# Four early loads of a fused attention and long-convolution kernel issued from ScalarE's queue

## The chip, the cores and the metric

The kernel runs on one core of a Trainium2 chip. A core has five engines, each with an instruction queue of its own that runs in order: TensorE (PE, with its weight loads as PEld), VectorE (DVE), ScalarE (ACT), GpSimd (POOL) and SyncE (SP, which only issues transfers here). Sixteen DMA engines move data between HBM and the core's memory. The metric is the device time of one execution in microseconds (us), as the median of several runs.

## The reference: what is computed

Two stages follow each other. The first is a linear attention with a decaying state, for 4 batches (B), 8 heads (H), 768 steps (S) and head size 48 (D):

```python
for t in range(S):
    kt, vt, rt, wt = k[:, :, t], v[:, :, t], r[:, :, t], w[:, :, t]
    cur = np.einsum('bhd,bhe->bhde', u[None] * kt, vt)
    y[:, :, t] = np.einsum('bhd,bhde->bhe', rt, state + cur)
    state = wt[:, :, :, None] * state + np.einsum('bhd,bhe->bhde', kt, vt)
```

Its output, laid out as 4 x 768 x 384, goes through the second stage:

```python
x1, x2, x3 = np.split(x @ w_proj, 3, axis=-1)
X2 = np.fft.rfft(x2, n=S, axis=1) * np.fft.rfft(filter_fft, n=S, axis=0)[None]
y = x1 * np.fft.irfft(X2, n=S, axis=1) * x3
out = y @ w_out
```

The inputs r, k, v and w are float32 in HBM, laid out batch, head, step, head size.

## The kernel before, in words

The 768 steps of each batch are cut into six chunks of 128 steps (L), which makes 24 chunks in all, numbered 0 to 23; chunks 0 to 5 belong to batch 0. For each chunk four loads bring r, k, v and w as 128 x 384 float32 (192 KB each, 8 x 128 pieces of 192 bytes) into rings of six buffers: ldr, ldk, ldv, ldw. All of them are made by `op_ld` (line 449, the issue at line 452).

What is done to a chunk c, with the names of the schedule:

- `lw` (line 457, ACT): the logarithm of w. `cs` and `ce` (lines 464 and 468, PE): its running sums, inclusive and exclusive of the step itself, as products with triangular masks. `en`, `eq`, `ph` (lines 483 to 495, ACT): the exponentials of those sums.
- `kh` and `q` (lines 501 and 504, DVE or POOL): k times en, and r times eq, into the buffer qk. `rk` (line 507): r times k.
- `rt` and `rT`, `tqk` and `tT` (PE, then DVE or ACT): transposes of rk and of qk and their copies out of PSUM. `sc` (line 601, PE): the scores of a chunk. `mt` (line 612, DVE): their mask. `cp` and `cc`, `vc`: the term with u. `kv` and `S` (lines 619 and 631): the state that goes on to the next chunk. `y`, `xn`, `yt`, `xT`: the output of the attention and its transpose.
- `um`, `ub`, `ubd`, `uc`, `rku`: what is made of u, whose 1.5 KB are loaded by `ldu`.

The second stage does the Fourier transforms as products with matrices of sines. These are computed at the start: the angles by `ang` and `and` (lines 329 and 347, DVE), the sines by `sin` (line 355, ACT), which loads ACT's table of sines before and the table of logarithms and exponentials after. The filter's spectrum follows (`fs`, `fd`, `hf`, `H`, `hg`), and then, batch by batch, projections (`p1`, `x2`, `p3`), spectra (`f`), products (`ur`, `ui`, `pp`), inverses (`iE`, `iO`, `iP`), gates (`g`, `yy`) and the output product (`po`, `o`), stored by `st`.

The order of all work is written out by hand in the string ORDER (lines 42 to 141). Each word names an engine and an operation: `A:` ACT, `V:` DVE, `P:` PE, `G:` POOL, `S:` SyncE. `emit` (line 864) takes the words one by one, so that each engine's queue has its own words in the order of the string. A number behind `@` is the PSUM bank, and one behind `+` a number of matmuls on a tile of zeros that PE runs ahead of the operation. The framework adds the semaphore waits. ACT's queue begins with

```python
A:tLn0 ... A:lw0 ... A:lw1 ... A:lw2 ... A:en1 A:eq0 ... A:lw4 ... A:en2 ... A:eq2 ... A:eq1 A:ph2 A:en0 ... A:ph1 ... A:sin ... A:v0 ... A:eq4 ... A:ph0 ... A:lw3 ... A:uc
```

where `tLn0` (line 352) loads ACT's table of logarithms. SyncE's queue begins with

```python
S:ldw0 S:ldk2 S:ldw1 S:ldr3 S:ldw2 S:ldu S:ldr0 S:ldw4 S:ldk1 S:ldk0 S:ldr1 S:ldw6 S:ldv2 S:ldr2 S:ldv0 S:ldk3 S:ldw3 S:ldr4 ...
```

and DVE's first products come in the order q0, rk0, kh0, q1, kh1, with the last of the angles between q0 and rk0. All transfers, the weights, the filter and the stores too, are issued by SyncE.

Of the kernel before, what the change touches and what calls it, by code (L numbers as in the profile page):

```python
# [19 lines left out]
B, H, S, D = 4, 8, 768, 48  # L20
# [19 lines left out]


ORDER = """
A:tLn0 S:ldw0 G:iota S:ldk2 S:ldw1 S:ldr3 G:mx V:late G:mi V:ang2 S:ldw2 G:uh A:lw0 S:ldu V:ang1
S:ldr0 P:ce0@0+2 S:ldw4 G:id A:lw1 V:ang0 S:ldk1 P:cs1@1+3 S:ldk0 P:cs0@2 G:nyq A:lw2 S:ldr1
V:and1 A:en1 P:ce2@3+4 A:eq0 S:ldw6 P:um@4 P:cs2@5 V:q0 P:ce1@1 A:lw4 V:and2 S:ldv2 A:en2 V:and0
A:eq2 P:ce4@5 S:ldr2 A:eq1 A:ph2 A:en0 V:rk0 P:ub@3 A:ph1 S:ldv0 A:sin V:kh0 P:rt0@2 V:q1
P:tqk0@1+1 S:ldk3 V:kh1 V:rT0 V:tT0 S:ldw3 P:tqk1@2 P:sc0@8+1 S:ldr4 V:rk2 G:q2 S:ldw5 G:rk1
# [97 lines left out]
def kernel(  # L145
# [12 lines left out]
    nc = tc.nc  # L158
# [83 lines left out]
    nyq = consts.tile([L, NT], FP32)  # L242
# [42 lines left out]
    def bi(c):  # L285
        return divmod(c, NCH)
# [162 lines left out]
    def op_ld(e, x, c):  # L449
        b, ci = bi(c)  # L450
        src = dict(w=w, k=k, r=r, v=v)[x]
        nc.sync.dma_start(  # L452
            out=ld[x][c % 6],
            in_=src[b, :, ci * L:ci * L + L, :].rearrange("h t d -> t h d"),
        )
# [476 lines left out]
```

## Time and profile before

| | |
|---|---|
| median of 3 runs | 156.67 us (156.21 to 157.68) |
| profiled execution, time | 157.1 us |
| profiled execution, span of its instructions | 155.4 us |
| mean granted TensorE clock | 0.973 of full speed |
| DMA moved | 28.98 MB, mean 186 GB/s over the span |
| loads of r, k, v, w | 24 of each, 192 KB each, median 3.9 to 4.2 us from issue to landing |

The profile is one execution, taken by the hardware profiler. A row of a timeline has the start and the length in us, the engine, the line of the kernel, the operation, what is written and read, and in brackets the idle time of the engine ahead of it with what ended that. SPq is SyncE's queue; the length of its rows is that of the issue and not of the transfer. A row of the windows has the busy time of each engine in that stretch, the clock that TensorE was granted, the mean busy share of the 16 DMA engines, and GB/s. The chain of work that ended last is followed back from the last instruction, at each step to what released it. Busy times of PE are modelled at their ends, and idle time of an engine that others don't wait for costs nothing.

### The profile page before, as it was taken

To read this page: it belongs to the slowest core of one execution; us is meant where nothing else is said; L and a number is where in the kernel's file an instruction comes from. 1 tells how busy PE (TensorE), PEld (TensorE's weight loads), DVE (VectorE), ACT (ScalarE), POOL (GpSimd) and SP (SyncE) were. 2 spreads that over 40 slices of the span, in tenths; PEclk is the share of its full clock that TensorE was granted. 3 is DMA by queue.
4 is the path that set the end of the run, shared out by engine and by line. 5 is a ranking of instruction groups with operands and counts; after the bars stand their busy time and mean duration, and the time that the engine had idled before them with its cause. 6 is when DMAs were issued, how large, how long until landed. Compare 5 with 4: busy or idle time off the path is not lost.

```text
span 155.4 us, 4177 instructions
## 1 busy us (share of the span) xinstructions
PE 144.5 (93%) x1540; PEld 90.8 (58%) x1540; DVE 138.3 (89%) x264; ACT 128.2 (82%) x306; POOL 115.9 (75%) x134
## 2 busy tenths in 40 slices
PE   6969988968999999999999999999999999999990
PEld 3446565756465666656757666775666566555440
DVE  6537879979989999999999999999999989999950
ACT  3279659969698899989999999999999877677470
POOL 7200869892999899799969999699999998900600
PEclk9985799999999999999999999999999999999997
DMA  5999979999999999899999999978999986000575
GB/s 96 196 202 183 207 148 197 195 286 226 244 172 281 253 178 200 170 192 211 190 200 259 170 181 210 189 147 141 227 209 228 206 175 222 2 0 0 181 281 203
DMA packets 112038, 28.98 MB, mean 186 GB/s; under 512 B 106641, under 2 KB 112018, under 8 KB 112018
## 3 DMA queue, kind: packets, MB, share of 16 engines
q1 hardware_dynamic: 112018, 28.72, 84.4%
q8 instruction: 12, 0.20, 0.6%
q14 instruction: 8, 0.07, 0.1%
HBM read 22.41 MB, written 4.72 MB: 175 GB/s over the span
## 4 chain that ended last, share of the span: by engine, by line
PE 63%; DMA 12%; DVE 11%; ACT 5%; SPq 5%; issue 2%; DVEq 0%
PE p L705 13%; DMA ldw<-in_w_dram 9%; PE x L735 6%; PE po L850 6%; PE f L421 5%; SPq L452 5%; PE sc L607 3%; PE f L413 3%; PE tqk L588 3%; DMA ldv<-in_v_dram 3%; PE iE L792 3%; PE iO L781 3%; PE iE L781 2%; PE yt L675 2%; DVE mt L614 2%
## 5 line engine op out<-in xcount | busy, mean ns | idle before, releaser
L505 POOL TENSOR_TENSOR qk<-ldr,eq 128x384 bf16<-128x384 f32 x20 | 21.3, 1067 | 11.4 <-ACT F L357 10.3
L705 PE MATMUL p<-xT,wproj 128*128 128x384 bf16 x144 | 29.3, 326 | 0.1
L614 DVE TENSOR_TENSOR mt<-sc,mask_excl 128x1024 bf16<-128x1024 f32 x24 | 29.2, 1216 | 0.0
L502 POOL TENSOR_TENSOR qk<-ldk,en 128x384 bf16<-128x384 f32 x21 | 22.4, 1067 | 4.1 <-PE kv L625 2.7
L508 POOL TENSOR_TENSOR rk<-ldr,ldk 128x384 bf16<-128x384 f32 x19 | 19.8, 1042 | 1.8 <-issue 1.5
L560 POOL TENSOR_TENSOR rku<-rk,u_bc 128x384 bf16<-128x384 bf16 x19 | 18.0, 945 | 2.5 <-DVE rk L508 1.3
L462 ACT ACTIVATE lg<-ldw 128x384 bf16<-128x384 f32 x24 | 12.6, 530 | 8.6 <-DMA ldw<-in_w_dram 7.5
L705 PEld LDWEIGHTS <-wproj 128*128 128x128 bf16 x144 | 13.0, 97 | 8.2 <-issue 1.0
L582 POOL TENSOR_TENSOR vc<-v,cc 128x384 bf16<-128x384 bf16 x19 | 16.5, 867 | 0.7 <-DVE cc L566 0.5
L757 DVE TENSOR_TENSOR filt<-f,HF 128x768 bf16<-128x768 f32 x18 | 16.6, 952 | 0.1
L735 PE MATMUL x<-wproj,sd 128*128 128x384 bf16 x72 | 14.9, 326 | 0.3 <-DVE HF L435 0.2
L276 ACT ACTIVATE qkT<-tqk 128x1024 bf16<-128x1024 bf16 x13 | 13.3, 1027 | 0.1
L276 ACT ACTIVATE v<-ldv 128x384 bf16<-128x384 f32 x23 | 12.2, 530 | 1.3 <-DMA ldv<-in_v_dram 1.3
L276 ACT ACTIVATE x<-p 128x384 bf16<-128x384 f32 x24 | 11.7, 499 | 1.8 <-PE p L705 1.6
L726 POOL TENSOR_TENSOR g<-g,x 128x384 bf16<-128x384 bf16 x8 | 7.1, 912 | 8.1 <-DVE g L278 8.1
L276 ACT ACTIVATE ab<-x 128x384 bf16<-128x384 f32 x24 | 11.7, 500 | 1.2 <-PE x L735 0.9
L484 ACT ACTIVATE en<-cs 128x384 f32<-128x384 f32 x24 | 11.9, 500 | 0.9 <-PE cs L466 0.7
L490 ACT ACTIVATE eq<-ce 128x384 f32<-128x384 f32 x24 | 11.5, 494 | 0.6 <-PE ce L478 0.6
L588 PE MATMUL tqk<-ident,qk 128*128 128x128 bf16 x144 | 11.5, 230 | 0.2 <-ACT phi L496 0.2
L632 DVE TENSOR_TENSOR S<-kv,phi 128x384 bf16<-128x384 f32 x20 | 10.9, 550 | 0.3 <-PE kv L625 0.2
L566 DVE TENSOR_REDUCE cc<-rku 128x8 f32<-128x384 bf16 x21 | 11.1, 541 | 0.0
L276 ACT ACTIVATE xT<-yt 128x384 bf16<-128x384 bf16 x20 | 9.9, 495 | 1.3 <-PE yt L675 0.6
(158 smaller groups left out, 397.0 us busy)
## 6 DMA issues: line engine op xcount, KB each, us to landing
ldw<-in_w_dram SPq DMA_DIRECT2D x24, 192.0 KB, 4.0
ldk<-in_k_dram SPq DMA_DIRECT2D x24, 192.0 KB, 4.2
ldr<-in_r_dram SPq DMA_DIRECT2D x24, 192.0 KB, 3.9
ldv<-in_v_dram SPq DMA_DIRECT2D x24, 192.0 KB, 4.0
out_dram<-o_all SPq DMA_DIRECT2D x24, 192.0 KB, 2.2
raw<-in_moe_w_proj_dram SPq DMA_DIRECT2D x3, 576.0 KB, 5.8
filt<-in_moe_filter_fft_dram SPq DMA_DIRECT2D x1, 1152.0 KB
P<-in_moe_w_out_dram SPq DMA_DIRECT2D x1, 576.0 KB, 5.0
```

What stands on the lines that cost most here:

```text
L276: nc.scalar.activation(out=o, in_=i, func=AF.Copy)
L462: nc.scalar.activation(out=o, in_=i, func=AF.Ln)
L502: two(e).tensor_mul(qk_b[c % 3][:, 1, :, 0:D], ld["k"][c % 6], en_b[c % 3])
L505: two(e).tensor_mul(qk_b[c % 3][:, 0, :, 0:D], ld["r"][c % 6], eq_b[c % 3])
L508: two(e).tensor_mul(rk_b[c % 2], ld["r"][c % 6], ld["k"][c % 6])
L560: two(e).tensor_mul(rku_b[c % 2], rk_b[c % 2], u_bc)
L582: two(e).tensor_mul(o, v, s.to_broadcast([L, H, D]))
L588: nc.tensor.transpose(p[:, x, j, :], qk_b[c % 3][:, x, 2 * j:2 * j + 2, :], ident)
L614: nc.vector.tensor_mul(mt_b[c % 3], bank_of[f"sc{c}"].rearrange("p q j t -> p (q j) t"), dataclasses.replace(m[:, :], ap=[m[:, :].ap[0], [ ...
L705: nc.tensor.matmul(p, wproj[:, cb, col0:col0 + L], xT_b[b % 2][:, cb, sl], start=(cb == 0), stop=(cb == CB - 1),)
L735: nc.tensor.matmul(p, sd_b[q][0][:, cb, ti * L:(ti + 1) * L], wproj[:, cb, C:2 * C], start=(cb == 0), stop=(cb == CB - 1),)
L757: two(e).tensor_mul(U_all[:, part, n], dataclasses.replace(f, ap=[f.ap[0], [0, 2]] + list(f.ap[1:])), HF[:, n, part:part + 2, :],)
```

## The change

Four of the words `S:ld..` are taken out of SyncE's order and written as `A:ld..` right behind the first word of the string, the load of ACT's table: r0, k1, k0, r1. They are ACT's first four instructions after that table load, ahead of lw0. `op_ld` issues a load from ScalarE's queue where the word's engine is A, and from SyncE's otherwise. All other words keep their order, and sources, destinations and sizes of all transfers are the same.

```diff
 ORDER = """
-A:tLn0 S:ldw0 G:iota S:ldk2 S:ldw1 S:ldr3 G:mx V:late G:mi V:ang2 S:ldw2 G:uh A:lw0 S:ldu V:ang1
-S:ldr0 P:ce0@0+2 S:ldw4 G:id A:lw1 V:ang0 S:ldk1 P:cs1@1+3 S:ldk0 P:cs0@2 G:nyq A:lw2 S:ldr1
+A:tLn0 A:ldr0 A:ldk1 A:ldk0 A:ldr1 S:ldw0 G:iota S:ldk2 S:ldw1 S:ldr3 G:mx V:late G:mi V:ang2 S:ldw2 G:uh A:lw0 S:ldu V:ang1
+P:ce0@0+2 S:ldw4 G:id A:lw1 V:ang0 P:cs1@1+3 P:cs0@2 G:nyq A:lw2 
 V:and1 A:en1 P:ce2@3+4 A:eq0 S:ldw6 P:um@4 P:cs2@5 V:q0 P:ce1@1 A:lw4 V:and2 S:ldv2 A:en2 V:and0
...
     def op_ld(e, x, c):
         b, ci = bi(c)
         src = dict(w=w, k=k, r=r, v=v)[x]
-        nc.sync.dma_start(
+        (nc.scalar if e == "A" else nc.sync).dma_start(
             out=ld[x][c % 6],
             in_=src[b, :, ci * L:ci * L + L, :].rearrange("h t d -> t h d"),
         )
```

## The prediction, made before the changed kernel ran

> **What bounds the kernel now.** I read the page first (busy shares, the slices), then the windows, the chain of work that ended last, and the timelines of SyncE's queue (SPq), ScalarE (ACT), VectorE (DVE) and TensorE (PE) over the first 44 us, because the diff touches only the first 10 us.
>
> ```profile
> span 155.4 us, 4177 instructions
> PE 144.5 (93%) x1540; PEld 90.8 (58%) x1540; DVE 138.3 (89%) x264; ACT 128.2 (82%) x306; POOL 115.9 (75%) x134
> ...
> DMA  5999979999999999899999999978999986000575
> ```
>
> Three engines and the DMA engines are each over four fifths busy. The windows (columns: length, busy us of PE, PEld, DVE, ACT, POOL, granted clock, DMA share, GB/s) split that by stage:
>
> ```profile
> 0.00:2.00 2.00, 0.81 (x3) 0.43 (x4) 1.09 (x11) 1.20 (x1) 1.21 (x9) 1.00 0.01 3
> 2.00:4.00 2.00, 1.94 (x8) 0.77 (x6) 1.62 (x12) 0.44 (x2) 1.72 (x9) 1.00 1.03 196
> 8.00:10.00 2.00, 1.72 (x19) 1.42 (x19) 0.98 (x3) 0.98 (x3) 0.00 (x0) 1.00 1.02 200
> 12.00:14.00 2.00, 2.00 (x9) 0.75 (x9) 1.99 (x5) 1.99 (x2) 0.00 (x0) 0.50 0.93 175
> 52.00:60.00 8.00, 8.00 (x83) 5.14 (x81) 7.97 (x11) 7.37 (x14) 6.97 (x7) 1.00 0.98 217
> ```
>
> The DMA engines are full from 2 us on, with 175 to 200 GB/s, while the compute engines have holes; from 52 us PE and DVE have none. So the end is set by how late the full stretch begins, and the start is fed by a saturated stream of loads. The chain agrees: at the start its long steps are loads, later VectorE, then TensorE.
>
> ```profile
> 3.79 3.65 DMA ldw<-in_w_dram
> ...
> 15.03 5.32 DMA ldw<-in_w_dram
> ...
> 28.04 4.31 DMA ldv<-in_v_dram
> ...
> 36.09 4.99 DMA ldw<-in_w_dram
> ...
> 43.30 0.75 DVE HF L440
> ...
> 49.27 0.34 PE yt L675 x3
> ```
>
> **The change part by part.** Four loads of 192 KB leave SyncE's queue (r0, then k1 and k0, then r1) and ScalarE issues them behind its first table load.
>
> ```profile
> 0.80 0.45 SPq L452 DMA_DIRECT2D ldw<-in_w_dram  x1
> ...
> 5.19 0.57 SPq L452 DMA_DIRECT2D ldr<-in_r_dram  x1
> 5.81 0.74 SPq L452 DMA_DIRECT2D ldw<-in_w_dram  x1
> 6.59 2.18 SPq L452 DMA_DIRECT2D ldk<-in_k_dram  x2
> 8.82 0.80 SPq L452 DMA_DIRECT2D ldr<-in_r_dram  x1
> ```
>
> ```profile
> 0.80 1.28 ACT L353 ACT_TABLE_LOAD   x1 [0.80 <-PEq L916]
> 3.65 0.52 ACT L462 ACTIVATE lg<-ldw 128x384 bf16<-128x384 f32 x1 [1.56 <-DMA ldw<-in_w_dram]
> ...
> 7.46 0.52 ACT L462 ACTIVATE lg<-ldw 128x384 bf16<-128x384 f32 x1 [1.45 <-DMA ldw<-in_w_dram]
> ...
> 9.77 0.52 ACT L462 ACTIVATE lg<-ldw 128x384 bf16<-128x384 f32 x1 [1.02 <-PE ce L478]
> ...
> 11.37 0.51 ACT L484 ACTIVATE en<-cs 128x384 f32<-128x384 f32 x1
> ...
> 11.97 1.28 ACT L357 ACT_TABLE_LOAD   x1
> ...
> 20.37 0.52 ACT L462 ACTIVATE lg<-ldw 128x384 bf16<-128x384 f32 x1 [2.24 <-DMA ldw<-in_w_dram]
> ...
> 32.37 0.52 ACT L276 ACTIVATE v<-ldv 128x384 bf16<-128x384 f32 x1 [1.33 <-DMA ldv<-in_v_dram]
> ...
> 41.10 0.52 ACT L462 ACTIVATE lg<-ldw 128x384 bf16<-128x384 f32 x1 [0.97 <-DMA ldw<-in_w_dram]
> ```
>
> *Removed from SyncE's queue:* 0.57 + 2.18 + 0.80 = 3.55 us of issuing. I give it no gain: those issues run in the shadow of the saturated stream, and the bytes ahead of w6 and all later loads stay the same. If the cover were gone, the loads from w6 on could come up to 3.55 us earlier.
>
> [...]
>
> *Added to ScalarE's queue:* four issues, at 0.45 us each (the first, unhindered) to 1.09 us each (the k pair). After the table load (ends 2.08) that is 1.8 to 4.4 us, so the first logarithm lw0 starts at 3.9 to 6.5 instead of 3.65. [...] Cost on the path: nothing, since lw1 and lw2 then wait for data longer than that (next step). [...]
>
> *Moved: the order in which loads land.* This is the main term. w2 is the fifth load now. lw0, lw1 and lw2 wait for loads one, three and five, and (7.46 - 3.65) / 4 = 0.95 us per load. In the changed kernel four loads enter beside SyncE's first four, and w2 comes behind all eight, ninth: 7.46 + 4 x 0.95 = 11.3 us if both queues begin together and share evenly. If ScalarE's first issue waits for the table load (2.08) and its data come 1.2 us later, at 3.3, then 1.3 of SyncE's loads pass alone (3.3 - 2.0, at 0.95 each), and w2, still sharing for most of its time, lands near 11.0. Bounds: 7.5 (SyncE's queue is served first) to 11.3; I take 11.2, because nothing in the trace prefers one queue. w4, seventh now, becomes tenth or eleventh counting by slots: about 12.2 to 12.6.
>
> [...]
>
> *What follows on ScalarE.* Behind lw2 stand, in order, en1, eq0, lw4, en2, eq2, eq1, ph2, en0, ph1 and the sine tables. en2 needs cs2, whose path on PE is:
>
> ```profile
> 8.39 0.82 PE L515 MATMUL um<-ones_f,u_row 1*128 1x1 f32 x6
> ...
> 9.15 0.34 PE L466 MATMUL cs<-lg,mask_incl 128*128 128x384 bf16 x1
> ...
> 16.45 3.82 PE L269 MATMUL cp<-warm 128*128 128x384 bf16 x20
> ```
>
> cs2 ends at 9.49, 2.03 us after lw2 starts, so at 13.2. en0 ends 1.68 us after the old en2 start at 10.20 (11.37 + 0.51 = 11.88), so at 14.9. If lw4 really waits for the end of PE's ce1, as its row says, the whole old distance from lw2 to en0 (4.42) stays and en0 ends at 15.6.
>
> *What follows on DVE and PE.*
>
> ```profile
> 9.02 0.56 DVE L505 TENSOR_TENSOR qk<-ldr,eq 128x384 bf16<-128x384 f32 x1 [2.73 <-DMA ldr<-in_r_dram]
> ...
> 12.02 0.56 DVE L508 TENSOR_TENSOR rk<-ldr,ldk 128x384 bf16<-128x384 f32 x1 [1.49 <-DMA ldk<-in_k_dram]
> 12.49 0.55 DVE L502 TENSOR_TENSOR qk<-ldk,en 128x384 bf16<-128x384 f32 x1
> ...
> 20.44 0.17 DVE L278 COPY cc<-cp 128x8 f32<-128x8 f32 x1 [0.96 <-PE cp L554]
> ...
> 34.07 1.02 DVE L505 TENSOR_TENSOR qk<-ldr,eq 128x384 bf16<-128x384 f32 x1 [0.97 <-ACT eq L490]
> ...
> 43.30 0.75 DVE L440 TENSOR_SCALAR HF<-HF 128x384 bf16<-128x384 bf16 x1 [0.53 <-ACT HF L433]
> ```
>
> The stalls that go are r0's (2.73 us) and k0's (1.49 us): both land by about 9.7. What is late next is eq0 and then en0: kh0, at 12.49 now, starts at 14.9 to 15.6, so 2.4 to 3.1 us later. I take 2.5, near the lower end, because ce1's matmuls do not feed lw4. From there to cc0 everything hangs on one thread (kh0, transposes, tT0, scores, 20 warming matmuls of 3.82 us, cp0, cc0), so cc0 comes 2.5 us later; its 0.96 us of waiting is for PE, which is late too, and absorbs nothing.
>
> *What is given back.* From 20.44 to 52 us DVE has two real holes, 0.97 and 0.53 us, behind loads (v4 through ScalarE, w9 through ScalarE's HF) whose landing the stream sets. ScalarE's own slack there is 1.33 and 0.97. So 2.5 - 0.97 - 0.53 = 1.0 us is left on DVE at 44 us, and behind it everything is full.
>
> *An added wait in SyncE's queue.* The framework gives the loads eight completion semaphores in turn in program order, so the ninth and later wait for the load eight before. In the new order w2, u, w4 and w6 wait for the landings of r0, k1, k0 and r1, with all later issues queued behind. If ScalarE starts at once, r1 is the eighth load and lands near 10.3 (3.65 + 7 x 0.95), and w6's packets follow w4's without a gap: nothing. If it starts after the table load, r1 lands near 11.3; w6, issued then, moves data 1.2 us later (the first issue is at 0.80, the DMA share rises at 2.0) at 12.5, not at 2.0 + 10 x 0.95 = 11.5: the stream stands idle about 0.9 us and everything from w6 lands that much later. This doesn't add to the 1.0 us: both meet at w9 and DVE's wait at 43.30, and the larger counts.
>
> **Sum.** -0 (SyncE's issues) + 0 (ScalarE's issues) + 2.5 (kh0) - 1.5 (holes) = +1.0 us, with 0.9 instead where the stream's gap decides. The profiled execution took 157.1 us (span 155.4 and 1.7 around it), so 158.1 for one like it; it stands 0.4 above the median of 156.67, and the median becomes 157.7, 0.7% more.
>
> **The rivals.**
> *Slower: SyncE starves behind the semaphores.* If the moved loads drain slower than an even share, or ScalarE's issues take 1.09 us each and more, r1 lands later than 11.3, and each us of that is a us without packets in a stream that has no slack (0.93 to 1.03). At 1.5 us beyond it, r1 at 12.8, w3, v4 and w9 land 2.4 us later, DVE's holes stay open, and the end moves by 2 to 3 us: 159.0 to 159.7. For it: three waits in a row in front of w6. Against: a pair of loads takes 1.9 us, and I see no reason for more. It decides from r1 landing after about 12.
> *No difference.* w2 lands near 7.5 to 9 (SyncE's queue served first), or PE's granted clock, 0.50 at 12 to 14 us now, is back at 1.00 before the later transposes and saves about 1 us of the delay. kh0 is late by 1.5 or less, the holes take all of it: 156.4 to 157.0. [...]
> *Faster.* Two queues fill gaps of the stream: if it ran at 200 instead of 175 GB/s in such windows, w3, v4 and w9 would land up to 1 us earlier, and kh0 could move from 12.49 to 11.88 (en0's end). 155.3 to 156.2. Against: w2's place in the order, and at most 0.07 of share is free in the windows above.
>
> **How the numbers follow.** The forecast (+0.5 to +1.5 us, 157.2 to 158.2) gets 0.55; the slower rival 0.27, no difference 0.12, faster 0.06. Predicted is 157.7. The range is from no difference to the starved stream, 156.3 to 159.6. A measurement of this kernel tells about 1% (1.6 us, from 155.1 to 158.2) from no change. Beyond that lie the slower rival and some of the forecast's upper end, 0.36; half of the faster rival, 0.04; the rest, 0.60, is within.
>
> **What would show it.** Right: lw2 waits for its load until about 11; DVE's waits for r0 and k0 are gone, and q0 waits for eq0; kh0 at 14.9 or later; cc0 near 23; the holes at 34 and 43 us smaller. The issues on ScalarE have rows of their own, and the one after the table load tells whether it waited. A DMA share below 0.8 in 11 to 13 us would be the semaphores' gap. Wrong: lw2 before 9; w3's logarithm much later than 21.5 (the slower rival) or before 20 (the faster one); a delay at cc0 that is still whole at 52 us would mean that the holes gave nothing back.

## The result and the profile after

The changed kernel takes 162.50 us (median of 4 runs, 162.16 to 162.56), the kernel before in the same rounds 157.18 us (156.21 to 158.32): a ratio of 1.033, with a 95% interval of 1.028 to 1.039. The prediction was 157.7 us with a range to 159.6; the change costs 5.3 us where 1.0 was forecast. The profiled execution took 162.47 us with a span of 160.3 (before 157.1 and 155.4), so it stands for the median. Ratios, here and below, leave disturbed runs out, so they are not always the quotient of the two medians.

The page of the changed kernel, its span and the clock's row in slices of 4 us each:

```profile
span 160.3 us, 4176 instructions
...
PEclk9955559999999999999999999999999999999999
```

and the clock's row on the page of the kernel before:

```profile
PEclk9985799999999999999999999999999999999997
```

The work is the same, but TensorE's granted clock is halved in four slices (8 to 24 us), before in some two. (In the first slice or two the row is no evidence for either kernel; the counter-test below says why.) The windows of the changed kernel show the start (columns as in the prediction):

```profile
2.00:12.00 10.00, 5.78 (x27) 2.49 (x25) 3.51 (x16) 2.06 (x6) 2.54 (x12) 0.77 1.31 219
```

```profile
8.00:10.00 2.00, 1.97 (x6) 0.84 (x6) 0.00 (x0) 0.00 (x0) 0.00 (x0) 0.50 1.41 217
10.00:12.00 2.00, 0.46 (x4) 0.18 (x3) 0.00 (x0) 0.93 (x3) 0.00 (x0) 0.50 1.30 207
...
20.00:24.00 4.00, 4.00 (x22) 1.87 (x21) 2.59 (x6) 2.81 (x6) 0.00 (x0) 0.50 0.93 181
```

The stream of loads is not starved: 219 GB/s from 2 to 12 us, where the same window of the kernel before has 197. The engines that compute are: from 8 to 10 us ACT, DVE and POOL have nothing at all to do (before, DVE and ACT have 0.98 us each), and PE's 1.97 us there are six matmuls at half rate. At 20 to 24 us the clock is still 0.50, with PE full. ScalarE's timeline tells why:

```profile
0.83 0.48 ACTq L452 DMA_DIRECT2D ldr<-in_r_dram  x1
1.34 2.02 ACTq L452 DMA_DIRECT2D ldk<-in_k_dram  x2
...
4.29 0.70 ACTq L452 DMA_DIRECT2D ldr<-in_r_dram  x1
5.04 0.52 ACT L462 ACTIVATE lg<-ldw 128x384 bf16<-128x384 f32 x1 [2.96 <-DMA ldw<-in_w_dram]
7.46 0.52 ACT L462 ACTIVATE lg<-ldw 128x384 bf16<-128x384 f32 x1 [1.89 <-DMA ldw<-in_w_dram]
11.07 0.52 ACT L462 ACTIVATE lg<-ldw 128x384 bf16<-128x384 f32 x1 [3.09 <-DMA ldw<-in_w_dram]
...
14.07 0.49 ACT L484 ACTIVATE en<-cs 128x384 f32<-128x384 f32 x1 [1.30 <-PE cs L466]
...
21.91 0.52 ACT L462 ACTIVATE lg<-ldw 128x384 bf16<-128x384 f32 x1
```

The four issues begin at 0.83, beside the table load (0.80 to 2.08, as before). The first logarithm starts at 5.04, right behind the fourth issue (4.29 + 0.70 = 4.99). Its row puts the idle time down to the load, but by the trace's semaphore records w0 had landed at 4.27; in the run below where ScalarE's issues stand behind lw0, lw0 starts at 3.67. The second and the third do wait for their loads, and lw2 starts at 11.07 instead of 7.46. The logarithm of w3 at 21.91, which waited 2.24 us for its load before, waits for nothing now: the load landed at 17.36 instead of 20.35, and the engine is late. The long steps at the start of the chain that ended last in the changed kernel:

```profile
4.44 6.61 DMA ldw<-in_w_dram
12.23 1.36 PE um L515 x6
15.81 0.62 DVE qk L502
16.43 1.27 DVE qk L505
17.70 1.09 DVE qk L502
19.30 1.01 PE tqk L588 x8
21.17 4.98 PE cp L269 x20
```

That is the whole story in order: the load of w2, `um` at half rate, kh0, then q1 and kh1 at more than twice their old length, transposes, and the twenty warming matmuls ahead of cp0 in 5 us instead of 3.82. The rows behind it, on DVE and on POOL, first in the kernel before:

```profile
12.96 0.55 DVE L505 TENSOR_TENSOR qk<-ldr,eq 128x384 bf16<-128x384 f32 x1
13.43 0.55 DVE L502 TENSOR_TENSOR qk<-ldk,en 128x384 bf16<-128x384 f32 x1
```

```profile
15.98 1.36 POOL L505 TENSOR_TENSOR qk<-ldr,eq 128x384 bf16<-128x384 f32 x1 [10.28 <-ACT F L357]
```

and in the changed one:

```profile
15.81 0.62 DVE L502 TENSOR_TENSOR qk<-ldk,en 128x384 bf16<-128x384 f32 x1 [1.46 <-ACT en L484]
16.35 1.35 DVE L505 TENSOR_TENSOR qk<-ldr,eq 128x384 bf16<-128x384 f32 x1
17.62 1.35 DVE L502 TENSOR_TENSOR qk<-ldk,en 128x384 bf16<-128x384 f32 x1
...
26.32 0.17 DVE L278 COPY cc<-cp 128x8 f32<-128x8 f32 x1 [3.63 <-PE cp L554]
...
47.70 0.42 DVE L440 TENSOR_SCALAR HF<-HF 128x384 bf16<-128x384 bf16 x1
```

```profile
15.97 1.31 POOL L508 TENSOR_TENSOR rk<-ldr,ldk 128x384 bf16<-128x384 f32 x1
17.25 1.31 POOL L502 TENSOR_TENSOR qk<-ldk,en 128x384 bf16<-128x384 f32 x1
```

kh0 is 3.32 us late (15.81 against 12.49), cc0 is 5.88 us late (26.32 against 20.44), and where DVE used to wait for w9 (43.30) it is 4.40 us late and waits no more. Deep in the full stretch the logarithm of one and the same chunk starts at 86.13 before and at 90.67 after:

```profile
86.13 0.55 ACT L462 ACTIVATE lg<-ldw 128x384 bf16<-128x384 f32 x1
```

```profile
90.67 0.55 ACT L462 ACTIVATE lg<-ldw 128x384 bf16<-128x384 f32 x1
```

This delay of 4.54 us stays within 0.01 us for all logarithms from 65 to 113 us and serves below as a measure that accidents behind it do not touch; it is called the steady delay.

### The profile page after: what moved, and what is told of

It is laid out like the page before. It is cut to its first block, busy times and chain, and to the rows that moved or that the text cites. A ratio compares the mean times of both kernels' runs of the same rounds, so it can differ in the third digit from the quotient of the medians.

```text
span 160.3 us, 4176 instructions
## 1 busy us (share of the span) xinstructions
PE 146.8 (92%) x1540; PEld 92.0 (57%) x1540; DVE 139.3 (87%) x264; ACT 128.0 (80%) x306; POOL 116.8 (73%) x134
## 4 chain that ended last, share of the span: by engine, by line
PE 70%; DMA 8%; ACT 7%; DVE 5%; issue 2%; SPq 2%; POOL 1%; ACTq 0%
PE p L705 12%; PE x L735 8%; PE po L850 5%; PE f L421 4%; PE sc L607 4%; DMA ldw<-in_w_dram 4%; PE tqk L588 4%; PE cp L269 3%; PE f L413 3%; PE iE L792 3%; PE yt L675 3%; PE iO L781 2%; PE y L646 2%; DMA ldk<-in_k_dram 2%; PE iE L781 2%
## 5 line engine op out<-in xcount | busy, mean ns | idle before, releaser
L502 POOL TENSOR_TENSOR qk<-ldk,en 128x384 bf16<-128x384 f32 x21 | 23.4, 1113 | 3.2 <-ACT phi L496 2.0
L462 ACT ACTIVATE lg<-ldw 128x384 bf16<-128x384 f32 x24 | 12.6, 530 | 7.9 <-DMA ldw<-in_w_dram 7.9
```

The costliest lines, as they stand in the source:

```text
L462: nc.scalar.activation(out=o, in_=i, func=AF.Ln)
L502: two(e).tensor_mul(qk_b[c % 3][:, 1, :, 0:D], ld["k"][c % 6], en_b[c % 3])
```

## The experiments

My theory after the result: the time is lost by the order in which the loads land, which puts w2 behind four others; from there it grows because TensorE's clock is cut for longer and because GpSimd's products now run beside DVE's. The rivals: the second queue does the harm (ScalarE's issuing, or the DMA engines shared by two queues), or one of the two amplifiers is an innocent bystander. All medians of the kernel before are from the same rounds. No kernel below leaves out any of the computation; warming matmuls work on zeros.

**The same order from one queue.** All loads on SyncE, in the order in which they land in the changed kernel:

```diff
-A:tLn0 A:ldr0 A:ldk1 A:ldk0 A:ldr1 S:ldw0 G:iota S:ldk2 S:ldw1 S:ldr3 ... S:ldw2
+A:tLn0 S:ldw0 S:ldr0 G:iota S:ldk2 S:ldk1 S:ldw1 S:ldk0 S:ldr3 S:ldr1 ... S:ldw2
```

> All loads on SyncE's queue again, in the order in which they landed in the changed kernel (w0 r0 k2 k1 w1 k0 r3 r1, then w2). If the order of the loads is the cause, lw2 starts at about 11 us as in the changed kernel, TensorE's clock is cut as long, and the time is 161.5 to 163.5 us. If ScalarE's queue or the use of two queues is the cause, it is back at 156.5 to 158.5 us.

Measured: 162.87 us (162.48 to 163.43) against 156.69, ratio 1.041 (1.033 to 1.049). Its cc0 comes at 25.72, and its lw2 is

```profile
11.05 0.52 ACT L462 ACTIVATE lg<-ldw 128x384 bf16<-128x384 f32 x1 [3.14 <-DMA ldw<-in_w_dram]
```

One queue in this order loses as much as two. The order is the cause, and the second queue is not needed for it.

**ScalarE issues the same four loads, but later.** r0 behind lw0, k1 and k0 behind lw1, r1 behind lw2:

```diff
-A:tLn0 A:ldr0 A:ldk1 A:ldk0 A:ldr1 S:ldw0 ... A:lw0 ... A:lw1 ... A:lw2
+A:tLn0 S:ldw0 ... A:lw0 A:ldr0 ... A:lw1 A:ldk1 A:ldk0 ... A:lw2 A:ldr1
```

> ScalarE issues the same four loads, but r0 behind lw0, k1 and k0 behind lw1, r1 behind lw2, about where SyncE issued them before. If the order is the cause, lw2 starts by 8.5 us and the time is 156.5 to 158.5 us. If issuing from ScalarE is the cause, the four issues of 0.5 to 1.3 us each still stand in ScalarE's queue, and the time is 160 us or more.

Measured: 157.66 us (156.58 to 158.26) against 156.69, ratio 1.006 (1.002 to 1.010).

```profile
8.33 0.52 ACT L462 ACTIVATE lg<-ldw 128x384 bf16<-128x384 f32 x1 [2.29 <-DMA ldw<-in_w_dram]
```

With the issues on ScalarE's queue and w2 only 0.87 us later than before (8.33 against 7.46), some four fifths of the loss are gone, and cc0 comes at 21.19. The queue costs at most the rest, about 1 us.

**Half of the move.** Only r0 and k0 go to ScalarE; k1 and r1 stay at their old places on SyncE:

```diff
-A:tLn0 A:ldr0 A:ldk1 A:ldk0 A:ldr1 S:ldw0
+A:tLn0 A:ldr0 A:ldk0 S:ldw0
```

> The changed kernel with only r0 and k0 on ScalarE's queue; k1 and r1 are back at their old places on SyncE's. w2 has two loads fewer ahead of it: if its place sets the start, lw2 begins at 9.0 to 9.6 us, cc0 comes at 22 to 23.5 us and the time is 158.3 to 160 us, about half of the loss. If any early load of ScalarE costs the whole, through the clock, 161.5 us or more; if VectorE's holes take it, 157.5 us or less.

Measured: 158.91 us (158.03 to 159.58) against 156.90, ratio 1.019 (1.005 to 1.032).

```profile
9.32 0.52 ACT L462 ACTIVATE lg<-ldw 128x384 bf16<-128x384 f32 x1 [1.26 <-DMA ldw<-in_w_dram]
```

Two loads ahead of w2 put lw2 back by 1.86 us, four by 3.61: 0.9 us for each, as the prediction's 0.95 had it.

**The changed kernel with more warming matmuls.** TensorE gets matmuls on zeros where it would wait for w0, w1, w2 and the exponentials:

```diff
-P:ce0@0+2 ... P:cs1@1+3 ... P:ce2@3+4 ... P:ce4@5 ... P:ub@3
+P:ce0@0+9 ... P:cs1@1+12 ... P:ce2@3+19 ... P:ce4@5+4 ... P:ub@3+4
```

> The changed kernel with more matmuls on zeros in the holes that TensorE has now: 9 instead of 2 ahead of ce0, 12 instead of 3 ahead of cs1, 19 instead of 4 ahead of ce2, 4 ahead of ce4 and of ub. Loads and all else as in the changed kernel. If the cut clock (0.50 from 7.4 to 24.4 us) multiplied the delay, the cut is shorter than 10 us, cc0 comes by 23.5 instead of 26.3 us and the time is 158.5 to 160.5 us. If the clock is a bystander, cc0 stays at 26 and the time is 162 to 163 us.

Measured: 160.87 us (159.94 to 162.84), ratio 1.026 (1.016 to 1.036), just beyond the 158.5 to 160.5 us expected. By the ratios that is not clear of the changed kernel's 1.033 (1.028 to 1.039); the rows are the evidence.

```profile
17.59 1.35 DVE L502 TENSOR_TENSOR qk<-ldk,en 128x384 bf16<-128x384 f32 x1
...
20.29 3.42 PE L269 MATMUL cp<-warm 128*128 128x384 bf16 x20
...
23.89 0.17 DVE L278 COPY cc<-cp 128x8 f32<-128x8 f32 x1 [1.36 <-PE cp L554]
```

The same twenty matmuls take 3.42 us instead of 5.05, cc0 comes 2.43 us sooner, and kh1 keeps its 1.35 us: the clock is one amplifier and leaves the other as it was. Nineteen matmuls ahead of ce2 were too many: the last of them ends after lw2 does, so kh0 is still at 15.78, and part of the gain may be lost there.

**The kernel before without its early warming matmuls.** The counter-test: does a cold start alone cost as much?

```diff
-P:ce0@0+2 ... P:cs1@1+3 ... P:ce2@3+4
+P:ce0@0 ... P:cs1@1 ... P:ce2@3
```

> The kernel before without the 2, 3 and 4 matmuls on zeros ahead of ce0, cs1 and ce2; loads as before. If the clock multiplies, it is cut from about 7 us to beyond 20 us though all loads come in time, and the time is 158.5 to 160.5 us. If the clock is a bystander, the time is within 0.5 us of the kernel before.

Measured: 157.66 us (156.90 to 158.41) against 156.69, ratio 1.009 (1.006 to 1.012). Neither expectation holds: the loss is 1.0 us by the medians and 1.4 by the ratio, more than nothing and less than the 2 to 4 us of a clock that explains it all.

```profile
8.60 1.43 PE L515 MATMUL um<-ones_f,u_row 1*128 1x1 f32 x6
...
16.77 4.45 PE L269 MATMUL cp<-warm 128*128 128x384 bf16 x20
```

`um` takes 1.43 us instead of 0.82, as it does at the half rate of the changed kernel, and the twenty matmuls take 4.45 us, between 5.05 in the changed kernel and 3.42 in the run above. The eight of sc0 just ahead of the twenty take 0.61 us, as at half rate in the changed kernel, so half rate ended among the twenty. cc0 (21.39) is 0.95 us late. In a start that is not late, half rate for that long costs no more than that. The page of this kernel, though, has

```profile
PEclk9999999999999999999999999999999999999998
```

so that row is no evidence for the first stretch of a run: it shows full speed here, where `um` takes 1.43 us. The duration of a matmul is the evidence.

**Both amplifiers off.** To the warming of above comes a wait: GpSimd reads two columns of kh1's result before it begins rk1, so that its rk1 and kh2 cannot run beside DVE's q1 and kh1. (Its q2, ahead of the wait, still can run beside kh0.)

```diff
-S:ldw5 G:rk1
+S:ldw5 G:hold G:rk1
...
+    def op_hold(e, k_):
+        nc.gpsimd.tensor_copy(out=held, in_=qk_b[1][:, 1, 0, 0:2])
```

> The changed kernel with the extra matmuls on zeros, and GpSimd made to wait for kh1 (a copy of two columns of qk, ahead of rk1), so that VectorE's q1 and kh1 run without GpSimd's rk1 and kh2 beside them. If that neighbourhood stretches VectorE's products (1.35 instead of 0.55 us), they fall to 0.55 us, cc0 comes at 22.5 to 23.2 instead of 23.9 us and the time falls to 159.5 to 160.4 us. If the length has another cause or is covered, q1 and kh1 stay at 1.35 us or the time stays at 160.5 to 161.5 us.

Measured: 158.18 us (158.04 to 160.75) against 156.75, ratio 1.014 (1.010 to 1.018).

```profile
15.06 1.07 DVE L503 TENSOR_TENSOR qk<-ldk,en 128x384 bf16<-128x384 f32 x1 [0.79 <-ACT en L485]
16.05 0.54 DVE L509 TENSOR_TENSOR qk<-ldr,eq 128x384 bf16<-128x384 f32 x1
16.52 0.55 DVE L503 TENSOR_TENSOR qk<-ldk,en 128x384 bf16<-128x384 f32 x1
...
22.04 0.17 DVE L279 COPY cc<-cp 128x8 f32<-128x8 f32 x1 [1.10 <-PE cp L558]
...
86.38 0.55 ACT L463 ACTIVATE lg<-ldw 128x384 bf16<-128x384 f32 x1
```

With the loads in the changed kernel's order, but the clock full and DVE alone in q1 and kh1, these take 0.55 us again, kh0 is 2.57 us late (15.06), cc0 only 1.60, and the steady delay is 0.25 us. That is better than the 22.5 to 23.2 us for cc0 and the 159.5 to 160.4 us expected. The order alone leaves 1.4 us by the medians and 2.2 by the ratio; the rest of the 5.3 us, three to four, is the two amplifiers. Not all that sets this run apart from the one with warming alone is GpSimd's wait: `um` starts at 12.19 us here and at 12.90 there, and kh0 starts 0.72 us earlier. (The profiled execution, at 158.09, is 1.0 us above that of before; the part beyond 0.25 arises behind 100 us and around the span and is not explained.)

**The wait on GpSimd alone.** The changed kernel with `hold`, and no more warming than it had:

```diff
-S:ldw5 G:rk1
+S:ldw5 G:hold G:rk1
```

> The changed kernel, with nothing else than GpSimd's wait for kh1 ahead of rk1. By the thread that leads to cc0, q1 and kh1 fall to 0.55 us each, but tqk0 at the half clock then ends last: tT0 comes 0.5 us earlier, cc0 at 25.8 instead of 26.3 us and the time is 161.5 to 162.3 us. If the neighbourhood costs by itself what it cost beside the full clock, cc0 comes 1.8 us earlier and the time is 159.5 to 160.8 us.

Measured: 159.56 us (159.27 to 161.09) against 156.90, ratio 1.026 (1.015 to 1.038).

```profile
17.56 1.91 PE L592 MATMUL tqk<-ident,qk 128*128 128x128 bf16 x16
...
20.09 3.42 PE L270 MATMUL cp<-warm 128*128 128x384 bf16 x20
...
23.68 0.17 DVE L279 COPY cc<-cp 128x8 f32<-128x8 f32 x1 [1.55 <-PE cp L558]
```

(By the ratios this, too, is not clear of the changed kernel; by the times all four are below its lowest.) This misses the 161.5 to 162.3 that I expected and falls where the rival put it, but by another way than that of DVE's products, which are 0.8 us shorter each. In the changed kernel the transposes of chunk 1 wait for rT0, which stands behind kh1 on DVE; PE stands still for 0.61 us in between, and the clock stays at half:

```profile
17.63 1.06 PE L588 MATMUL tqk<-ident,qk 128*128 128x128 bf16 x8
19.30 1.01 PE L588 MATMUL tqk<-ident,qk 128*128 128x128 bf16 x8 [0.61 <-DVE rkT L278]
...
21.10 5.05 PE L269 MATMUL cp<-warm 128*128 128x384 bf16 x20
```

With kh1 in time the 16 transposes run back to back, the clock is full again near 19.8 us (sc0's eight matmuls, from 19.73, take 0.43 us, where they take 0.61 in the changed kernel at half rate and 0.40 with warming at full rate) instead of at 24.45 by the trace's record of its changes, and the twenty matmuls take 3.42 us. Up to that rise PE's rows show no gap from 16.17 us on; in the changed kernel they show the one of 0.61 us ahead of 19.30. That the pause kept the clock at half is my inference from these rows, not shown by itself: the clock's steps lie at other places in the two executions, and that may be part of the difference. So the two amplifiers are not separate terms: each taken away alone brings cc0 forward by about 2.5 us (to 23.89 and 23.68), both together by 4.28. How much belongs to which can't be said.

**The changed kernel without the twenty warming matmuls** ahead of cp0:

```diff
-P:cp0@1+20
+P:cp0@1
```

> The changed kernel without the 20 matmuls on zeros ahead of cp0. If cc0 is late because those matmuls run at the cut clock on the one thread that feeds it, cc0 comes at 22 to 23 instead of 26.3 us, and the time is 159 to 160.5 us. If TensorE needs them to get the clock back, the cut lasts longer than to 24.4 us, what follows is slower, and the time stays at 162 us or goes above.

Measured: 160.59 us (159.45 to 161.24) against 156.75, ratio 1.021 (1.015 to 1.027).

```profile
22.54 0.15 DVE L278 COPY cc<-cp 128x8 f32<-128x8 f32 x1
```

```profile
24.00:28.00 4.00, 3.82 (x45) 2.83 (x42) 3.60 (x7) 3.34 (x10) 2.93 (x4) 0.50 0.85 160
```

cc0 comes 3.78 us sooner than in the changed kernel, the time is only 1.9 us less. Without them the clock is still half at 24 to 28 us, but that is not where most of the gain goes: the logarithm of w9 starts 3.34 us sooner still (41.70 against 45.04), and the steady delay is 2.20 us, 2.34 sooner. The rest is lost behind 41 us; the profiled execution, at 161.24, is also the slowest of its four. In this late kernel the twenty cost more than they bring.

**The loads in the order of their use, on one queue.** If the order is what counts, w0, w1, w2 first should bring cc0 forward (the loads alone, without the words in between):

```diff
-S:ldw0 S:ldk2 S:ldw1 S:ldr3 S:ldw2 S:ldu S:ldr0 S:ldw4 S:ldk1 S:ldk0 S:ldr1 S:ldw6 S:ldv2 S:ldr2 S:ldv0 S:ldk3 S:ldw3
+S:ldw0 S:ldw1 S:ldw2 S:ldr0 S:ldw4 S:ldu S:ldk0 S:ldk1 S:ldr1 S:ldr2 S:ldk2 S:ldv0 S:ldw3 S:ldr3 S:ldk3 S:ldw6 S:ldv2
```

> The kernel before with SyncE's first loads in the order of their use: w0 w1 w2 r0 w4 u k0 k1 r1 r2 k2 v0 w3 r3 k3 w6 v2. If the place of w2 and w4 among the loads sets the start, lw2 starts by 6 us, kh0 by 10.5 instead of 12.5 us and cc0 by 18.5; how much of it reaches the end depends on the landing of v4 and w9, which stays: 154.5 to 156.5 us. If the order of loads matters only when w2 is late, the time is 156.5 to 157.5 us.

Measured: 156.74 us (154.26 to 157.83) against 156.75, ratio 0.998 (0.995 to 1.002): no difference, with cc0 0.75 us sooner (19.69). (The profiled execution was the fastest of ten, 154.26, and towards its end 2.8 us ahead of the profile of before; it does not stand for the median.) **Nearly the same order with r0, k1, k0 and r1 on ScalarE,** behind lw0, lw1 and lw2 (on SyncE u is now ahead of w4, and k2 ahead of r2):

```diff
+... A:lw0 A:ldr0 ... A:lw1 A:ldk1 A:ldk0 ... A:lw2 A:ldr1
```

> The same order of use, with r0, k1, k0 and r1 issued by ScalarE behind lw0, lw1, lw1 and lw2. If two queues at once move more (207 to 235 GB/s in the changed kernel from 2 to 12 us where the kernel before had 186 to 202), the loads behind land about 1 us earlier than with one queue and the time is 153.5 to 155.5 us. If the second queue brings nothing, it is within 0.7 us of the same order on one queue.

Measured: 157.47 us (157.11 to 159.98), ratio 1.006 (1.001 to 1.010). The second queue brings nothing in this order either. **One queue, order of use, and GpSimd's wait:**

```diff
-S:ldw5 G:rk1
+S:ldw5 G:hold G:rk1
```

> The loads in the order of use on SyncE's queue, and GpSimd made to wait for kh1. kh1 falls from 1.35 to 0.55 us, cc0 comes at 19.0 to 19.5 instead of 19.7 us; 156.0 to 157.0 us, as the loads of v4 and w9 take up the rest. If VectorE's thread alone sets the end, 155.5 us or less.

The diff stands against the kernel with the loads in order of use. Measured: 156.28 us (155.59 to 156.93) against 156.90, ratio 1.000 (0.996 to 1.004).

```profile
16.65 0.17 DVE L279 COPY cc<-cp 128x8 f32<-128x8 f32 x1 [1.36 <-PE cp L558]
```

```profile
20.90 0.52 ACT L463 ACTIVATE lg<-ldw 128x384 bf16<-128x384 f32 x1 [2.63 <-DMA ldw<-in_w_dram]
```

cc0 is 3.79 us sooner than in the kernel before, and nothing comes of it: the logarithm of w5, the next behind that of w3, waits 2.63 us for its load, where it waited for nothing before. From here the stream of loads sets the pace. **The same with `um` moved behind ce4,** four warming matmuls ahead of ce4 and of rt0, and eight instead of twenty ahead of cp0:

```diff
-P:um@4 P:cs2@5 ... P:ce4@5 ... P:ub@3 ... P:rt0@2 ... P:cp0@1+20
+P:cs2@5 ... P:ce4@5+4 ... P:um@4 P:ub@3 ... P:rt0@2+4 ... P:cp0@1+8
```

> The same, with TensorE's um behind ce4 instead of ahead of cs2, 4 matmuls on zeros ahead of ce4 and rt0, and 8 instead of 20 ahead of cp0. If the thread to cc0 is what the start costs, en2 comes 0.7 us earlier, cc0 by 17.5 us, and the time is 154 to 156 us. If TensorE's clock needs the 20, it is cut for longer than 7 us and the time is 156.5 us or more; if the later loads hold the end, it stays at 156 to 157 us with cc0 early.

Measured: 157.16 us (155.97 to 159.37), ratio 1.004 (0.999 to 1.009). cc0 is sooner still (15.99) and w5's wait longer (3.25 us).

No version beat the kernel before. A cc0 sooner than its 20.44 us brought nothing in the medians; a later one cost, by the medians, between 0.7 and 1.8 times its delay: 0.9 times in the changed kernel, 1.2 times with its order on one queue.

## Why the prediction was wrong

*SyncE's queue gains nothing from 3.55 us fewer issues:* right for the time, but the reason was not. The stream had room (219 GB/s for 197), and the loads behind came sooner, w3 by 3.0 us; no engine was ready for them.

*ScalarE's issues cost nothing on the path:* right. lw0 started at 5.04, inside 3.9 to 6.5, behind the fourth issue, which ended at 4.99; lw1 and lw2 then waited 1.89 and 3.09 us for data. Who issued made little difference: 162.87 us with one queue, 162.50 with two, in the same order.

*w2 lands as ninth load:* right, 11.05 for 11.2, and w4 at 11.95 for 12.2 to 12.6. The two queues shared evenly here: k1, w1, k0, r3, r1 and w2 land at 6.53, 7.44, 8.34, 9.25, 10.15 and 11.05, one of ScalarE's and one of SyncE's in turn.

*en2 at 13.2, kh0 2.5 us late:* the right mechanism, short by 0.8 us. en2 came at 14.07 because cs2 stands behind `um` on PE, and `um` took 1.43 us at half rate. With the clock full kh0 was 2.57 us late (15.06).

*"From there to cc0 everything hangs on one thread (kh0, transposes, tT0, scores, 20 warming matmuls of 3.82 us, cp0, cc0), so cc0 comes 2.5 us later":* this is the step that failed. It moved the thread as if it had a fixed length. It went from 7.95 us (20.44 - 12.49) to 10.51 (26.32 - 15.81), and with both amplifiers off it was 6.98 (22.04 - 15.06). Of the 2.56 us more, 1.33 arise ahead of the twenty matmuls (they start 5.29 us behind kh0 instead of 3.96) and 1.23 from there to cc0. I named the clock only as a possible gain, "back at 1.00 before the later transposes"; the same row, 0.50 at 12 to 14 us, also meant that a later start could lengthen the cut (by the trace's records it lasted 17.07 us instead of 6.83), and that had no price. That GpSimd's products could come to lie beside DVE's had no place in the sum: in the kernel before the first of them started at 15.98, 2 us after kh1 had ended.

*The holes give 1.5 us back:* nearly right for the changed kernel. From cc0 to 86 us its delay shrinks by 5.88 - 4.54 = 1.34 us, and by 1.60 - 0.25 = 1.35 with both amplifiers off. It is no constant of the kernel, though: with the order on one queue and in the counter-test the delay shrinks by 0.3 us only, and without the twenty matmuls not at all. In the counter-test two of DVE's HF records, from 45.77 us, take 2.03 us together instead of the 1.29 of the same two before; what stretched them stays open.

*SyncE's semaphores open a gap of up to 0.9 us,* and the slower rival made of it: neither happened. The stream ran at 219 GB/s, not slower. By the trace's records w2's issue (4.44) waited for no semaphore; r1's did, on ScalarE, for w0's, and began at 4.29, right behind w0's landing at 4.27. The side of that rival was the right one, its mechanism was not; its sum of 159.0 to 159.7 was too low as well (2 to 3 us on 156.67 give 158.7 to 159.7).

The sum as it came out: 3.32 (kh0) + 2.56 (the thread) - 1.34 (holes) = 4.54 us at 86 us. The rest, 162.47 - 157.1 - 4.54 = 0.8 us, arises half in the span behind 86 us and half around the span; that is less than the runs of the kernel before differ among themselves (156.21 to 158.32).

Open: how the loss divides between clock and neighbour, since they act on each other, and how much of either is the place of the clock's steps in one execution; why 197 GB/s went through in the first 12 us before and 213 in the other order on the same single queue:

```profile
2.00:12.00 10.00, 5.60 (x28) 2.52 (x26) 3.51 (x16) 2.08 (x6) 2.55 (x12) 0.87 1.08 213
```

## What to carry to other kernels

Here, where the engines wait for a stream of loads at the start, a load moved to ScalarE's queue was above all a load moved forward, and what it passed was late by 0.9 us for each 192 KB; rank the first loads by when they are used, whoever issues them. Moving them further forward still brought nothing where the wait went over to another load, as in the runs with the loads in the order of their use (156.74 us against 156.75). The delay at the start of this tuned schedule was not a shift of the whole (3.32 us at kh0, 5.88 at cc0, 4.54 at 86 us): price each step behind such a delay at the clock and beside the neighbours that it will then have. Check the half-rate clock by the length of a known matmul (here `um`, 1.43 us for 0.82), and price it in both directions.

## What the runs showed of the hardware

TensorE's clock changes, by the trace's records, at 3.97, 7.38 and 24.45 us in the changed kernel and at 7.06, 10.47 and 17.30 before. The distances are 3.41 and 17.07 us, and 3.41 and 6.83: in these two executions each is a multiple of 3.41 us (one and five, one and two). Half rate is the second of each pair: 17.07 us in the changed kernel and 6.83 in the kernel before. What sets the step was not shown. Ahead of the first record the lengths of matmuls tell: the three warming matmuls ahead of cs1 took 1.12 us from 5.08 before, and 0.65 us from 5.91 in the changed kernel.

In the changed kernel DVE's and GpSimd's products end in turn: at 16.43 (DVE kh0), 17.28 (POOL rk1), 17.70 (DVE q1), 18.56 (POOL kh2) and 18.97 (DVE kh1), by start plus length in the rows above. That is 0.85 us from an end of DVE's to the next of POOL's, and 0.42 from there to the next of DVE's. With GpSimd's wait, which keeps rk1 and kh2 from running beside them, q1 and kh1 take 0.55 us each instead of 1.35, and rk1 takes 1.00 instead of 1.31. That the two engines wait for each other is read from these ends and lengths; no row shows the wait itself.

With two queues, in the windows of 2 us from 4 to 12 us of the changed kernel, the DMA share reads 1.30 to 1.41 for 207 to 235 GB/s. From 2 to 12 us it reads 1.31 for 219 GB/s with two queues, and 1.08 for 213 with one queue in the same order: the share is a fifth higher, the bytes 3%.
